# A list schedule that plans itself again from its own deadlines, with four products of the first pair moved ahead of the pair and the fillers written into the next operation's bank

## The chip, the cores and the metric

One NeuronCore of a Trainium2 chip runs the whole kernel. The metric is the device time of one execution in microseconds; three executions of the kernel before took 883.96 (median), 883.89 and 884.6 us. The engines are TensorE (PE: matrix products into PSUM; PEld is its weight load, which overlaps), VectorE (DVE), ScalarE (ACT), GpSimd (POOL) and SyncE (SP), whose queue issues every DMA here. Each engine runs its instructions in the order in which they were written and waits for the others by semaphores.

## The reference

Attention with pooled keys and values, followed by a two-layer gated network over all tokens:

```python
# 8 batches, 8 heads, 576 tokens, head_dim 64; q, k, v float32
k_p = k.reshape(B, H, 72, 8, D).mean(axis=3); v_p = v.reshape(B, H, 72, 8, D).mean(axis=3)
scores = np.matmul(q, k_p.transpose(0, 1, 3, 2)) / np.sqrt(D)
scores = scores - np.max(scores, axis=-1, keepdims=True)
attn = np.exp(scores); attn = attn / (np.sum(attn, axis=-1, keepdims=True) + 1e-09)
x = np.matmul(attn, v_p)            # then (tokens, heads*D) = (4608, 512)
h = x @ w_in                        # w_in (512, 2048), w_out (2048, 512)
sp = np.maximum(h, 0.0) + np.log1p(np.exp(-np.abs(h)))
out = (h * erf(sp)) @ w_out
```

## The kernel before

**Numbers.** The products of the network are made from limbs: a float32 matrix is cut into a high part and the rest, and one product is three matmuls (high x high, high x low, low x high; the helper `three`, line 687). The weights arrive as words of 64 bits where they are given so and are turned into float32 by ScalarE or GpSimd (`cv`, `low`), VectorE (lines 397 and 399, `cv` and `f`) and cut into `w` limbs (`halves`: the high part on ScalarE or GpSimd, line 340 or 341, the rest on VectorE or GpSimd, line 352).

**Tiling.** The 4608 tokens are nine chunks of 512. Chunk 0 goes through plain products: sixteen blocks of 128 of the hidden dimension, each 12 matmuls of 128x512 (`plain_in`), then `second`, 192 matmuls into four output banks. Chunks 1 to 8 go in four pairs, s = 1 to 4. In a pair the first layer runs in eight quads (`quad`): a quad makes four 128x512 blocks of h for both chunks from seven products of six matmuls by a scheme of Strassen and Winograd. Its moving operands are differences of the two chunks' x (T1, T2, T3, T4) beside x itself (B11, B21, B22), made in `sides` as limbs; its weights are blocks of w_in (`w`) and their sums (`ws`, made in `sums`). For the first pair seven of the eight products A11 x B11 are made ahead by `head`, which leaves p1 in SBUF, since they need only the first chunk of the pair. In a quad with a p1 the product A12 x B21 has its own bank and is added to p1 on VectorE (`add(g[0, 0], p1, A)`).

**Activation.** `activation` takes four blocks: softplus of each on ScalarE out of PSUM (line 697), erf of the four in two instructions (line 701), then the product with h (line 705 or 708). Softplus lies in another function table than erf and sigmoid, so ScalarE loads a table between them. In the plain stage the multiplication of line 708 is the last reader of the bank, so the bank is free for another block when it is done.

**Attention.** For each tile of up to 128 tokens: scores (PE line 520), maximum and difference (DVE 529, 545), a sigmoid that stands for the exponential (ACT 539 or 549), the sum and its reciprocal (551 to 555), scaling (561, 565), transposes (PE 572, 575), values (PE 615, 616), and x out of PSUM; chunk 0 is cut into limbs at once (ACT 633, DVE 635). Keys and values are pooled on VectorE (line 470: `ks` and `vs`).

**What sets the order.** Nothing is written in the order in which it runs. Every operation is handed to `Program.op` with an engine (some with a second choice), a modelled cost, a priority (a due time from constants like `FIRST`, `LONG`, `PERIOD`) and the buffers that it holds; `Program.order` is a list schedule over that model. At each step it looks at every operation whose inputs are planned, works out its start on its engine, prefers small `start + SLACK * prio`, takes the earliest of the five engines' picks and gives its new buffers the place that came free first: 8 banks of PSUM (at most 6 for h, 4 for o, 4 for attention), 87 places of 2 KB in SBUF with a limit for each kind, such as 12 for `gl` or 14 for `w`. The instructions are then written in that order, so the order on every engine and every reuse of a place is fixed before the chip runs; a place that a slow store still holds makes the next user wait.

**Fillers.** Where the plan leaves PE idle in the first 57 us, small matmuls of constants (128x256, bfloat16) are written, of 107 ns in the plan, into one bank that is kept aside for them until 57 us:

```python
spare = heapq.heappop(slots["bank"])
...
idle = start - max(free["PE"], 3000.0) - MARGIN - (1800 if not free["PE"] else 0)
out.extend([self.filler] * int(idle / 107))
```

## Time and profile before

| | |
|---|---|
| median of three executions | 883.96 us |
| the profiled execution, its own time | 884.53 us |
| its span, first to last instruction | 882.5 us |
| mean granted TensorE clock | 0.992 |
| PE busy | 852.9 us (97%) |
| VectorE, ScalarE, GpSimd busy | 713.5, 561.6, 437.9 us |
| matmuls of the network (three groups: o; h by w; h by ws) | 1584 + 1344 + 192 |
| fillers | 178, 24.0 us |
| table loads of ScalarE | 36 + 28 + 8 + 1, 1283 ns each |

How to read it: busy times overlap, and an engine that is 97% busy leaves 29.6 us of the span to be won, as far as its work itself does not change; fillers count as busy, though they compute nothing. Idle time of the other engines counts only where PE waits for them. In a row of the timeline the first two numbers are start and length in us, the last bracket is the idle time of the engine just before and what ended it. In a row of groups the numbers behind the bar are busy us and mean ns of one.

### The profile page before, as it was taken

Reading aid. Unit: us, or ns where it says so; the run is one execution under the profiler, and the core shown is the slowest. Engines: PE = TensorE matmul, PEld = TensorE weight load, DVE = VectorE, ACT = ScalarE, POOL = GpSimd, SP = SyncE. Lnnn points to the kernel's source line nnn. Section 1 sums busy time; section 2 is a strip of 40 time slices with the busy share of each in tenths; the row PEclk is TensorE's granted clock in tenths of the full one; section 3 lists DMA queues with packets and bytes.
Section 4 is the critical chain, followed back from the end, with each engine's and each line's share of the span. In section 5 each row is a group of like instructions: output and inputs, shape, how many; then the busy total and the mean of one; then the engine's idle time right before and its main releaser. Section 6 shows DMA issues by size and latency. Waiting matters only on the chain. (4 is left out here: it accounts for less than half of the span.)

```text
span 882.5 us, 13579 instructions
## 1 busy us (share of the span) xinstructions
PE 852.9 (97%) x4106; PEld 701.0 (79%) x4106; DVE 713.5 (81%) x1264; ACT 561.6 (64%) x1002; POOL 437.9 (50%) x453
## 2 busy tenths in 40 slices
PE   8989899979899999999999999999999999999998
PEld 6777788768778888888887888888888888888886
DVE  5978779868888889578999998889898984567982
ACT  4778867648964475268766734587867445887630
POOL 1777578436856883035485333155474312484210
PEclk9999999989999999999999999999999999999999
DMA  8677999799898959997474367974633679448541
GB/s 286 228 243 243 295 353 321 253 375 383 294 340 315 374 196 375 353 355 268 141 267 146 119 204 262 352 238 121 227 120 120 203 268 350 118 121 266 175 163 52
DMA packets 125207, 218.03 MB, mean 247 GB/s; under 512 B 16976, under 2 KB 31440, under 8 KB 125136
## 3 DMA queue, kind: packets, MB, share of 16 engines
q1 hardware_dynamic: 125136, 217.18, 72.2%
q8 instruction: 33, 0.54, 0.3%
q14 instruction: 38, 0.31, 0.1%
HBM read 167.84 MB, written 49.28 MB: 246 GB/s over the span
## 5 line engine op out<-in xcount | busy, mean ns | idle before, releaser
L687 PE MATMUL o<-gl,w 128*128 128x512 f32 x1584 | 377.0, 393 | 1.6 <-DVE gl L352 1.4
L687 PEld LDWEIGHTS o<-gl,w 128*128 128x128 f32 x1584 | 292.7, 188 | 63.5 <-DVE gl L352 1.8
L687 PE MATMUL h<-x,w 128*128 128x512 f32 x1344 | 319.1, 394 | 7.5 <-DVE g L708 3.0
L687 PEld LDWEIGHTS h<-x,w 128*128 128x128 f32 x1344 | 250.9, 189 | 62.1 <-DVE g L708 3.2
L340 ACT ACTIVATE gl<-g 128x512 fp32r<-128x512 f32 x204 | 119.7, 624 | 74.9 <-DVE g L833 32.0
L352 POOL TENSOR_TENSOR gl<-g,gl 128x512 fp32r<-128x512 f32 x77 | 108.1, 1410 | 66.8 <-ACT gl L340 62.3
L705 POOL TENSOR_TENSOR g<-d,g 128x512 f32<-128x512 f32 x54 | 69.8, 1310 | 107.6 <-ACT d L701 93.8
L352 DVE TENSOR_TENSOR gl<-g,gl 128x512 fp32r<-128x512 f32 x139 | 107.6, 807 | 0.4 <-ACT gl L340 0.2
L770 DVE TENSOR_TENSOR g<-t,h 128x512 f32<-128x512 f32 x96 | 65.6, 684 | 41.0 <-PE h L687 39.9
L701 ACT ACTIVATE d<-d 128x1024 f32<-128x1024 f32 x72 | 72.7, 1051 | 0.3
L833 POOL TENSOR_TENSOR g<-g 128x512 f32<-128x512 f32 x48 | 67.3, 1413 | 8.8 <-DVE gl L352 6.1
L697 ACT ACTIVATE d<-g 128x512 f32<-128x512 f32 x103 | 57.5, 622 | 5.3 <-DVE g L770 5.2
L770 DVE TENSOR_TENSOR t<-t,h 128x512 f32<-128x512 f32 x57 | 39.1, 686 | 24.1 <-PE h L687 22.7
L687 PE MATMUL h<-x,ws 128*128 128x512 f32 x192 | 49.0, 410 | 6.8 <-DVE x L352 4.5
L561 POOL TENSOR_TENSOR bb<-s,z 128x64 f32<-128x64 f32 (+1 forms) x40 | 12.9, 322 | 81.1 <-DVE z L555 26.6
L687 PEld LDWEIGHTS h<-x,ws 128*128 128x128 f32 x192 | 38.1, 200 | 16.5 <-issue 6.3
L340 ACT ACTIVATE x<-xr 128x512 fp32r<-128x512 f32 (+2 forms) x64 | 34.4, 559 | 25.1 <-DVE xr L661 12.0
L615 PE MATMUL att<-et,va 128*128 128x256 f32 (+3 forms) x192 | 46.1, 340 | 1.4 <-DVE g L708 0.6
L520 PE MATMUL att<-kbd,q 128*128 128x144 f32 (+1 forms) x320 | 46.3, 287 | 1.2 <-issue 0.7
L520 PEld LDWEIGHTS att<-kbd,q 128*128 128x128 f32 (+1 forms) x320 | 42.2, 179 | 6.1 <-issue 2.2
L697 ACT ACT_TABLE_LOAD x36 | 46.2, 1283 | 0.6
L549 ACT ACTIVATE s<-s,cst 128x576 f32<-128x576 f32 (+1 forms) x36 | 27.9, 775 | 25.0 <-DVE s L545 24.8
(92 smaller groups left out, 1153.4 us busy)
## 6 DMA issues: line engine op xcount, KB each, us to landing
w<-ws SPq DMA_DIRECT2D x192, 256.0 KB, 4.8
w<-wo SPq DMA_DIRECT2D x136, 256.0 KB, 3.8
w<-wi SPq DMA_DIRECT2D x96, 256.0 KB, 5.0
ws<-ws SPq DMA_DIRECT2D x64, 256.0 KB, 5.3
v<-vl SPq DMA_DIRECT2D x48, 256.0 KB, 5.3
raw<-kl SPq DMA_DIRECT2D x32, 288.0 KB, 4.3
out<-f SPq DMA_DIRECT2D x36, 256.0 KB, 2.1
q<-qa SPq DMA_DIRECT2D x32, 256.0 KB, 5.1
```

The source lines that it names most:

```text
L340: op("ACT", act(n), prio, lambda: nc.scalar.activation(dst(), src(), AF.Copy, scale=scale), *access, turn=turn, alt=("POOL", 0.833 * n + 1 ...
L352: both(True, dve(n), gps(n), prio + 0.1, lambda e: e.tensor_sub(lo(), src(), f32(hi())), reads + [hikey], [lokey])
L520: nc.tensor.matmul(o, raw.ap[:, p, :T], kbd[:, p], start=(p % 2 == 0), stop=True, skip_group_check=True)
L549: op("ACT", act(H * SP) + 93, r + 0.8, lambda: nc.scalar.activation(s.ap[:T], s.ap[:T], AF.Sigmoid, bias=bias[0][:T], scale=1.0 / 64.0), [ ...
L561: nc.gpsimd.tensor_mul(bb.ap[:T], sv, zv.unsqueeze(2).broadcast_to([T, NP, 16]))
L615: nc.tensor.matmul(o, va[:, p], et.ap[:, p, :n], start=e == 0, stop=False, skip_group_check=True)
L687: nc.tensor.matmul(o, u, v, start=first and q == 0, stop=last and q == 2, skip_group_check=True)
L697: nc.scalar.activation(y(k), h.ap, AF.Softplus)
L701: op("ACT", act(1024), prio + 0.2, lambda k=k: nc.scalar.activation(ys[k].ap, ys[k].ap, AF.Erf), own[2 * k:2 * k + 2], own[2 * k:2 * k + 2 ...
L705: both(True, dve(512), gps(512), prio + 0.3, lambda e, k=k, h=h: e.tensor_mul(h.ap, y(k), h.ap), [own[k], h], [h])
L770: op("DVE", dve(512), prio, lambda: nc.vector.tensor_add(dst.ap, u.ap, o.ap), [u, o], [dst])
L833: both(True, dve(512), gps(512), prio, lambda e: e.tensor_sub(out.ap, u.ap, v.ap), [u, v], [out])
```

## The change

It has five parts.

1. *Passes.* `order` runs the list schedule up to eight times. After a pass, `latest` walks back from the planned end and finds for every operation the latest time at which it could end without moving that end, by its consumers, by the next operation on its engine and by the next user of its place; the latest start, divided by 5100 ns, is the operation's priority in the next pass. The pass with the shortest planned length is kept.
2. *Necks.* For four quads of the first pair the product A12 x B21 is made ahead, right after the heads (`neck`), and added to p1 in front of the quad; the quad then lacks that product and that add.
3. *Fillers.* No bank is kept aside. A filler goes into the bank that the next operation will take, from when that bank is free in the plan, in the first 57 us and later wherever the plan leaves PE idle for over 1.2 us.
4. *Softplus in twos.* The four softplus of `activation`, one operation before, are two operations of two.
5. A place keeps the operation that freed it, for the deadlines of part 1.

```diff
+PASSES, UNIT = 8, 5100.0
-HEADS = 7
+HEADS, NECKS = 7, 4
-FILL, MARGIN = 57000.0, 300
+FILL, MARGIN, LONG_IDLE = 57000.0, 300, 1200.0
...
+    def latest(self):
+        for o in self.ops:
+            o.late = self.length
+        for o in sorted(self.ops, key=lambda o: -o.start):
+            at = o.late - o.cost
+            for d, flow in o.next:
+                gap = self.DELAY[o.eng] if d.eng != o.eng else (self.SAME[o.eng] if flow else 0)
+                at = min(at, d.late_at - gap - o.cost)
+            for d, gap in o.after:
+                at = min(at, d.late_at - gap - o.cost)
+            o.late_at = at
+
+    def order(self, passes=PASSES):
+        best = None
+        self.prios = [o.prio for o in self.ops]
+        for n in range(passes):
+            self.reset()
+            try:
+                out = self.once()
+            except RuntimeError:
+                break
+            if best is None or self.length < best[0]:
+                best = (self.length, out, [(o.eng, o.cost, o.fn, o.start) for o in self.ops],
+                        [(b, b.place) for o in self.ops for b in o.bufs])
+            self.latest()
+            for o, p in zip(self.ops, self.prios):
+                o.prio = o.late_at / UNIT
...
-        spare = None
-        if self.filler:
-            spare = heapq.heappop(slots["bank"])
-            self.idle.place = spare[1]
...
+            if o.eng == "PE":
+                new = [b for b in o.bufs if b.home == "bank" and not b.held]
+                idle = start - max(free["PE"], 3000.0) - (1800 if not free["PE"] else 0)
+                if new and (start < FILL or idle > LONG_IDLE):
+                    begin = max(free["PE"], 4800.0 if not free["PE"] else 0.0, slots["bank"][0][0])
+                    out.extend([(self.filler, new[0])] * int((start - begin - MARGIN) / 107))
...
-        def softplus():
-            for k, (h, _) in enumerate(hs):
-                nc.scalar.activation(y(k), h.ap, AF.Softplus)
-
-        op("ACT", 4 * act(512), prio, softplus, [h for h, _ in hs], own, funcs="softplus")
+        for i in (0, 2):
+
+            def softplus(i=i):
+                for k in (i, i + 1):
+                    nc.scalar.activation(y(k), hs[k][0].ap, AF.Softplus)
+
+            op("ACT", 2 * act(512), prio + 0.01 * i, softplus, [h for h, _ in hs[i:i + 2]], own[i:i + 2], funcs="softplus")
...
+    def neck(s, i, x, due, p1):
+
+        a12 = piece(lambda: in_hbm[i][:, 1], IN[i], due)
+        A, g = bank("h"), place("g")
+        product(A, a12, "B21", x, due, False, True)
+        op("DVE", dve(512), due + 0.3, lambda: nc.vector.tensor_add(g.ap, p1.ap, A.ap), [p1, A], [g])
+        return g
...
-        if early:
+        if early and not g00:
             next(A, a12, "B21", False, True)
             add(g[0, 0], p1, A, due + 1.7)
...
+        g00s = [neck(s, i, x, start(s) - 0.5, ps[i]) for i in range(NECKS if s == 1 else 0)]
```

In numbers of instructions: the products and the attention are the same on PE, fillers are 240 instead of 178, ScalarE's table loads 97 instead of 73; the `gl` copies on ScalarE are 186 instead of 204 and on GpSimd 30 instead of 12; copies of `t` out of PSUM are 22 on VectorE instead of 10 and 3 on ScalarE instead of 15. GpSimd has 499 instructions instead of 458. The DMAs are the same 807 issues, in another order.

Where it moves instructions that the prediction speaks of, the rows of the program on one engine. Line numbers of the changed kernel are some 54 to 65 higher than those of the kernel before. First VectorE at the end of the start, up to the last limbs of chunk 0's x, before:

```order
L589 TENSOR_TENSOR etb<-att,etb 32x128 x2
L397 SCALAR_TENSOR_TENSOR cv<-cv,low 128x512
L470 TENSOR_REDUCE ks<-raw 128x72
L399 SCALAR_TENSOR_TENSOR f_688<-d,cv 128x512
L635 TENSOR_TENSOR x<-att,x 128x256 x2
L397 SCALAR_TENSOR_TENSOR cv<-cv,low 128x512
L470 TENSOR_REDUCE vs<-v 128x64
L399 SCALAR_TENSOR_TENSOR f_721<-d,cv 128x512
L635 TENSOR_TENSOR x<-att,x 128x256 x2
```

and now (583 and 599 are maximum and difference of the fifth tile, 689 the limb of x):

```order
L583 TENSOR_REDUCE m<-att 64x4 x2
L451 SCALAR_TENSOR_TENSOR cv<-cv,low 128x512
L599 TENSOR_TENSOR s<-att,m 64x288
L453 SCALAR_TENSOR_TENSOR f_775<-d,cv 128x512
L599 TENSOR_TENSOR s<-att,m 64x288
L451 SCALAR_TENSOR_TENSOR cv<-cv,low 128x512
L689 TENSOR_TENSOR x<-att,x 128x256 x2
L453 SCALAR_TENSOR_TENSOR f_806<-d,cv 128x512
L524 TENSOR_REDUCE vs<-v 128x64
L689 TENSOR_TENSOR x<-att,x 128x256
L451 SCALAR_TENSOR_TENSOR cv<-cv,low 128x512
L689 TENSOR_TENSOR x<-att,x 128x256
```

From the first four limbs of x to the last one, three pooled `vs`, three `cv`, two `f`, two maxima and two differences of the fifth tile have come in between; a `ks`, a limb of `w` and a scaling are no longer there, and one more `ks` stands ahead of the first four.

Second SP's queue with the loads of v (for `vs`) and of w_in, before:

```order
L386 DMA d<-wi 128x1024 x2
L467 DMA v<-vl 128x512 x2
L386 DMA d<-wi 128x1024 x7
L512 DMA q<-qa 128x512
L386 DMA d<-wi 128x1024 x2
L467 DMA v<-vl 128x512
L467 DMA raw<-kl 128x576
L386 DMA d<-wi 128x1024
L467 DMA v<-vl 128x512
```

and now:

```order
L521 DMA v<-vl 128x512
L566 DMA q<-qa 128x512
L440 DMA d<-wi 128x1024 x2
L521 DMA raw<-kl 128x576 x2
L521 DMA v<-vl 128x512
L566 DMA q<-qa 128x512
L440 DMA d<-wi 128x1024
L521 DMA v<-vl 128x512
L440 DMA d<-wi 128x1024
L521 DMA v<-vl 128x512
```

The tenth load of v, the first one in the last three rows of before and the second one here, has fourteen loads of w_in ahead of it in the queue before and five now.

Third PE just ahead of the first pair's quads, before (T2 is the first product by `ws`; the pair of 615 and 616 stands twice):

```order
L687 MATMUL h<-x,w 128x512 x24
L615 MATMUL att<-et,va 128x128
L616 MATMUL att<-etb,vb 64x128
L687 MATMUL h<-x,ws 128x512 x18
L687 MATMUL h<-x,w 128x512 x12
```

and now (the last two rows, a filler, stand 25 times, and then the T2 product follows):

```order
L741 MATMUL h<-x,w 128x512 x12
L669 MATMUL att<-et,va 128x128
L670 MATMUL att<-etb,vb 64x128
L741 MATMUL h<-x,w 128x512 x24
L669 MATMUL att<-et,va 128x128
L670 MATMUL att<-etb,vb 64x128
L1001 LDWEIGHTS cst
L1001 MATMUL h<-cst 128x256
```

66 matmuls of the first pair stand ahead of T2 now instead of 42, the last values of the attention directly ahead of the fillers.

More of the change, by code (lines that the diff above doesn't have):

```diff
@@ L180, in op, with reset, once @@
         return o
-    def order(self):
+    def reset(self):
+        for o in self.ops:
+            if not hasattr(o, "first"):
+                o.first = (o.wait, o.eng, o.cost, o.fn)
+            o.wait, o.eng, o.cost, o.fn = o.first
+            o.ready, o.done, o.before = 0.0, False, []
+            for b in o.bufs:
+                b.left, b.held, b.end, b.last = 0, False, 0.0, None
+        for o in self.ops:
+            for b in o.bufs:
+                b.left += 1
+    def latest(self):
+        for o in self.ops:
+            o.late = self.length
[22 more added lines that the diff above has]
+                o.prio = o.late_at / UNIT
+        self.length, out, how, places = best
+        for o, h in zip(self.ops, how):
+            o.eng, o.cost, o.fn, o.start = h
+        for b, p in places:
+            b.place = p
+        return out
+    def once(self):
+        for o in self.ops:
+            o.after = []
+        last, porter = {}, None
         free = {e: 0.0 for e in self.DELAY}
@@ L185, in order @@
         port = 0.0
-        slots = {t: [(0.0, i) for i in range(n)] for t, n in self.capacity.items()}
+        slots = {t: [(0.0, i, None) for i in range(n)] for t, n in self.capacity.items()}
         avail = {e: [] for e in free}
@@ L239, in order @@
             loaded = o.set or loaded
-            if spare is not None and o.eng == "PE":
-                if start > FILL:
-                    heapq.heappush(slots["bank"], (start, spare[1]))
-                    spare = None
-                else:
-                    idle = start - max(free["PE"], 3000.0) - MARGIN - (1800 if not free["PE"] else 0)
-                    out.extend([self.filler] * int(idle / 107))
+            if o.eng == "PE":
[4 more added lines that the diff above has]
+                    out.extend([(self.filler, new[0])] * int((start - begin - MARGIN) / 107))
             end = free[o.eng] = start + o.cost
@@ L249, in order @@
                 port = end
+            if o.eng in last:
+                last[o.eng].after.append((o, 0))
+            last[o.eng] = o
             o.done = True
@@ L256, in order @@
                     b.held = True
-                    b.places = {t: heapq.heappop(slots[t])[1] for t in b.limits}
+                    b.places = {}
+                    for t in b.limits:
+                        _, b.places[t], by = heapq.heappop(slots[t])
+                        if by is not None and by is not o:
+                            by.after.append((o, 150 + (DGE if e == "SP" else 0)))
                     b.place = b.places[b.home]
                 b.left -= 1
-                b.end = max(getattr(b, "end", 0.0), end)
+                if end >= b.end:
+                    b.end, b.last = end, o
                 if not b.left:
                     for t in b.limits:
-                        heapq.heappush(slots[t], (b.end + 150, b.places[t]))
+                        heapq.heappush(slots[t], (b.end + 150, b.places[t], b.last))
             for d in o.follow:
@@ L748, in head, with quad @@
         return p1
-    def quad(s, i, x, base, p1=None):
+    def neck(s, i, x, due, p1):
[4 more added lines that the diff above has]
+        return g
+    def quad(s, i, x, base, p1=None, g00=None):
         due = base + LONG / NQ * i
@@ L758, in quad @@
         s2, s3, s1 = sm(1), sm(2), sm(0)
-        a12 = piece(lambda: in_hbm[i][:, 1], IN[i], due)
+        if g00 is None:
+            a12 = piece(lambda: in_hbm[i][:, 1], IN[i], due)
         a22 = piece(lambda: in_hbm[i + NQ][:, 1], IN[i + NQ], due)
         s4 = sm(3)
-        A, Bk, C, Dk = (bank("h") for _ in range(4))
+        A, Bk, C, Dk = (None if m == 0 and g00 else bank("h") for m in range(4))
         n = [0]
@@ L773, in quad @@
         fts = (i, i + NQ)
-        g = {(m, t): place("g") for m in range(2) for t in range(2)}
+        g = {(m, t): g00 if g00 and m + t == 0 else place("g") for m in range(2) for t in range(2)}
         if not early:
@@ L919, in moe_attention @@
         ps = [head(s, i, x, start(s) - 1) for i in range(HEADS if s == 1 else 0)]
+        g00s = [neck(s, i, x, start(s) - 0.5, ps[i]) for i in range(NECKS if s == 1 else 0)]
         for i in range(NQ):
-            quad(s, i, x, start(s), ps[i] if i < len(ps) else None)
+            quad(s, i, x, start(s), ps[i] if i < len(ps) else None, g00s[i] if i < len(g00s) else None)
         span = SHORT if s < NC // 2 else 16
@@ L932, in moe_attention @@
             seconds(s, start(s) + LONG, span)
-    idle = bank("h")
     cb = c.bitcast(mybir.dt.bfloat16)
-    pr.idle = idle
-    pr.filler = Op("PE", 107, 0, lambda: nc.tensor.matmul(
-        idle.ap[:, :256], cb[:, :P], cb[:, :256], start=True, stop=True))
+    pr.filler = lambda b: nc.tensor.matmul(b.ap[:, :256], cb[:, :P], cb[:, :256], start=True, stop=True)
     ops = pr.order()
@@ L941, in moe_attention @@
     for o in ops:
-        o.fn()
+        if isinstance(o, tuple):
+            o[0](o[1])
+        else:
+            o.fn()
 def kernel(q, k, v, moe_w_in, moe_w_out):
```

## The prediction

> **What bounds the kernel now.** I read the page's busy times first, then a table of windows cut where TensorE's work changes kind, then TensorE's own timeline, then the engines on which it waits.
>
> ```profile
> span 882.5 us, 13579 instructions
> PE 852.9 (97%) x4106; PEld 701.0 (79%) x4106; DVE 713.5 (81%) x1264; ACT 561.6 (64%) x1002; POOL 437.9 (50%) x453
> 0.00:40.70 40.70, 35.23 (x263) 28.35 (x263) 29.21 (x69) 24.75 (x101) 18.21 (x32) 1.00 0.76 262
> 40.70:94.10 53.40, 49.08 (x216) 39.56 (x215) 43.00 (x78) 40.33 (x60) 38.44 (x44) 0.97 0.76 241
> 94.10:176.20 82.10, 76.88 (x396) 62.39 (x394) 69.27 (x143) 57.73 (x126) 54.46 (x65) 1.00 0.91 309
> 176.20:181.00 4.80, 0.48 (x2) 0.19 (x2) 2.73 (x9) 1.54 (x5) 0.00 (x0) 0.73 1.04 350
> 181.00:257.00 76.00, 72.14 (x300) 58.31 (x301) 61.21 (x103) 60.35 (x86) 48.41 (x51) 0.95 0.97 345
> 257.00:878.00 621.00, 618.75 (x2938) 512.17 (x2936) 506.96 (x866) 376.94 (x629) 278.37 (x263) 1.00 0.67 227
> ```
>
> The columns are window, length, then busy time of PE, PEld, DVE, ACT and POOL, then granted clock, DMA share and GB/s. From 257 us to 878 us PE is busy 618.75 of 621.00 us: nothing is to be won there, and the new order has the same products in the same places, so I leave it alone. What can move lies before 257 us: a start of 40.7 us in which PE waits for the first attention and mostly runs fillers, 4.3 us idle in the first GEMM (53.40 - 49.08), 5.2 us in the next stage, of which the last 1 us belongs to the wait that follows, 4.3 us in that wait, 3.9 us in the quads of the first pair, and some half clock. The rows that end these waits:
>
> ```profile
> 38.88 2.03 PE L937 MATMUL h<-cst 128*128 128x256 bf16 x17
> 40.67 16.61 PE L687 MATMUL h<-x,w 128*128 128x512 f32 x72
> 57.11 1.14 PE L520 MATMUL att<-kbd,q 128*128 128x144 f32 x8
> 61.24 10.06 PE L687 MATMUL h<-x,w 128*128 128x512 f32 x36 [2.99 <-DVE g L708]
> ...
> 176.16 0.50 PE L687 MATMUL h<-x,ws 128*128 128x512 f32 x1 [0.96 <-ACT x L340]
> 180.99 1.62 PE L687 MATMUL h<-x,ws 128*128 128x512 f32 x3 [4.32 <-DVE x L352]
> ...
> 231.87 2.00 PE L687 MATMUL h<-x,w 128*128 128x512 f32 x6 [2.31 <-DVE t L770]
> ```
>
> The first 72 matmuls take 57.11 - 40.67 = 16.44 us, 0.228 us each; seventeen fillers take 40.67 - 38.88 = 1.79 us, 0.105 us each. Each long wait is followed by a clock of one half for about 3.4 us or twice that:
>
> ```profile
> 61.20:64.60 3.40, 3.36 (x10) 2.72 (x11) 3.40 (x6) 3.38 (x6) 3.18 (x4) 0.66 0.97 363
> 181.00:184.00 3.00, 2.79 (x6) 1.79 (x7) 2.25 (x10) 1.03 (x3) 0.00 (x0) 0.50 1.07 388
> 231.60:235.00 3.40, 3.13 (x10) 2.49 (x11) 3.16 (x6) 3.37 (x5) 3.40 (x8) 0.70 0.42 124
> ```
>
> A clock share missing is time lost: 53.4 x 0.03 = 1.7 us after the first wait; 76.0 x 0.05 = 3.8 us in the quads, of which 3.0 x 0.50 and a tail of 0.6, 2.1 us, come from the wait at 181 us and 1.7 us from that at 232 us. The 36 matmuls behind the first wait confirm it: 10.06 us against 36 x 0.228 = 8.2 us.
>
> **Step 1, the start: +4.0 us.** The last limb of chunk 0's x releases the first GEMM, and VectorE is busy without a gap from the first four limbs to the last:
>
> ```profile
> 29.47 1.41 DVE L635 TENSOR_TENSOR x<-att,x 128x256 fp32r<-128x256 f32 x4
> 40.03 0.75 DVE L635 TENSOR_TENSOR x<-att,x 128x256 fp32r<-128x256 f32 x2
> L470 DVE TENSOR_REDUCE vs<-v 128x64 f32<-128x512 f32 x48 | 31.6, 674 | 3.2 <-DMA v<-vl 3.1
> L470 DVE TENSOR_REDUCE ks<-raw 128x72 f32<-128x576 f32 x32 | 23.8, 747 | 9.6 <-DMA raw<-kl 9.5
> L397 DVE SCALAR_TENSOR_TENSOR cv<-cv,low 128x512 uint32<-128x512 uint32 x32 | 22.0, 692 | 3.8 <-ACT cv L389 3.3 <-POOL low L395 0.2
> L399 DVE SCALAR_TENSOR_TENSOR f<-d,cv 128x512 uint32<-128x512 uint32 x32 | 21.5, 677 | 0.2
> L529 DVE TENSOR_REDUCE m<-att 64x4 f32<-64x288 f32 x16 | 6.8, 441 | 2.0 <-PE att L520 1.8
> L545 DVE TENSOR_TENSOR s<-att,m 64x288 f32<-64x288 f32 x16 | 6.6, 440 | 0.0
> L565 DVE TENSOR_TENSOR s<-s,z 128x576 f32<-128x576 f32 x25 | 26.3, 1051 | 0.9 <-POOL bb L561 0.8
> L352 DVE TENSOR_TENSOR w<-f,w 128x512 fp32r<-128x512 f32 x12 | 11.0, 915 | 4.7 <-POOL w L341 4.5
> ```
>
> In the new order three vs, three cv, two f, two m and two s more stand between the same two points: 3 x 0.674 + 3 x 0.692 + 2 x 0.677 + 2 x 0.441 + 2 x 0.440 = 7.2 us. One ks, one w and one s x z are gone: 0.747 + 0.915 + 1.051 = 2.7 us. That is +4.5 us; as the next instruction starts some 0.08 us before a listed end, nine more make it 3.8, and one ks more ahead of the first limbs and the s x z on GpSimd can add a little. I take 4.0, between 2 (fillers already held the first GEMM back by up to 1.8 us) and 6. Nothing hides it: PE has only fillers there, 34 more of them (3.6 us), which fill this gap and don't cause it. The work that was pulled ahead is late nowhere afterwards; it is what step 2 needs.
>
> **Step 2, first GEMM: -4.5 us.** Its 3 us wait is for bank space, and the profile shows why the bank came late:
>
> ```profile
> 49.78 1.28 ACT L697 ACT_TABLE_LOAD   x1
> 51.08 2.06 ACT L697 ACTIVATE d<-h 128x512 f32<-128x512 f32 x4
> 54.98 2.01 ACT L701 ACTIVATE d<-d 128x1024 f32<-128x1024 f32 x2
> L389 ACT ACTIVATE cv<-d 128x512 f32<-128x512 f32 x32 | 20.3, 635 | 3.5 <-issue 1.4 <-DVE xr L347 1.3 <-DVE s L545 0.5
> 59.90 0.69 DVE L470 TENSOR_REDUCE vs<-v 128x64 f32<-128x512 f32 x1 [3.08 <-DMA v<-vl]
> 60.51 2.47 DVE L708 TENSOR_TENSOR g<-d,h 128x512 f32<-128x512 f32 x4
> ```
>
> The multiplies (line 708) that free the banks were done on ScalarE's side at 57.0 us, but stood on VectorE behind a vs whose load sat on SP's queue behind fourteen loads of wi, which wait for their own slots; in the new order it sits behind five. And the first softplus pair starts after two products (of twelve matmuls each), not four. Worked by hand from 44.7 us on: two products end at 50.2; two softplus (1.2), a cv (0.6), a load (1.3) and an erf (1.0) end near 54.3; the 19 instructions that VectorE has between the last limb and these multiplies, some 0.6 us each, end near 56.6, two multiplies at 58. The first bank is wanted again after six products, at 61.1. So the 4.3 us of waits and 1.7 us of half clock go, -6.0. Back come 1.5 us: ScalarE now loads its table 14 times in this stage, not 8, 6 x 1.283 = 7.7 us, against 53.40 - 40.33 = 13.1 us that it was idle, and the first o products need four banks at once just behind the last activations. Ends: 0 to 5 us for that.
>
> [...]
>
> **Step 3, 94 to 176 us: 0.** The same products and attention, reshuffled; its 4 us of small waits may go or double, -4 to +4. Over the whole run eighteen gl copies move from ScalarE to GpSimd, at
>
> ```profile
> L341 POOL TENSOR_SCALAR gl<-g 128x512 fp32r<-128x512 f32 x12 | 15.0, 1252 | 18.4 <-DVE gl L352 12.1 <-PE att L575 5.0 <-PE att L520 0.8
> ```
>
> 22 us on an engine that is half idle, with twelve gl slots as a cushion; a gl that is late after all holds back six o matmuls.
>
> **Step 4, the wait for T2: -4.1 us.** What the first pair's products wait for are sides made from the last attention values. PE now has four more products (24 matmuls x 0.228 = 5.5 us) ahead of this point, but also ahead of the last values, so they don't fill the wait itself; they give VectorE time to be further on. In the old run two slots of SBUF came late:
>
> ```profile
> 180.08 0.96 DVE L352 TENSOR_TENSOR x<-xr,x 128x384 fp32r<-128x384 f32 x3 [2.07 <-DMA wf<-f]
> 181.44 0.72 ACT L340 ACTIVATE x<-xr 128x384 fp32r<-128x384 f32 x2 [3.62 <-DMA wo<-w]
> L770 DVE TENSOR_TENSOR g<-t,h 128x512 f32<-128x512 f32 x96 | 65.6, 684 | 41.0 <-PE h L687 39.9 <-DMA w<-ws 0.7
> ```
>
> Without them 5.5 us of wait (0.96 + 4.32 + 0.20) become some 3.5, the copy, two differences and two limbs of the last block. I take -2.0, from 0 (other stores hold slots) to -2.5. Then the 25 fillers, 25 x 0.105 = 2.6 us, leave under 1 us idle, and the half clock behind it goes: -2.1, or 0 if the fillers end early. VectorE's four neck adds (684 ns each by the last row, 2.7 us) stand ahead of the last T2 limb; they have their inputs before the last value and run in the wait, and where they don't they cost these 2.7.
>
> Waits of 2.99 and 2.31 us have halved the clock here (0.66 and 0.70 behind them), so if the fillers end 2 us early the 2.1 are lost and the sum is -5.2. [...]
>
> **Step 5, quads: -2.7 us.** 3.9 us of waits and 1.7 us of clock, where VectorE reached an add late among long multiplies. Four quads are one product and one add shorter, 5.5 us and 2.7 us, which moved ahead; but ScalarE, busy 60.35 of 76.00 us, has the same activations and two or three loads more. I take half, from -5.4 to +3.
>
> **Sum:** 4.0 - 4.5 + 0 - 4.1 - 2.7 = -7.3 us on a span of 882.5, 875.2. The profiled execution took 884.53 us, 0.57 above the median of the runs, 883.96, from which the same -7.3 gives **876.7 us**.
>
> **The rivals.** *The waits come back* (0.13): the start costs 4.0, the first GEMM wins 4.5, but T2 waits for slots as long as before, the fillers end ahead of it, and VectorE is as late in the quads: steps 4 and 5 are 0, 883.5 us. For it: the stores are the same, at a DMA share of 1.04 in that window. Against it: their queue positions and slots all differ.
>
> *ScalarE's loads set the pace* (0.17): the slower side. Each pair of softplus has its own two loads, and from the point where two products (12 matmuls each, 5.5 us) are shorter than a pair's work on ScalarE, 2 x 1.283 + 2 x 0.6 + 1.0 + two cv of 0.6 = 6.0 us, banks come late again. Step 2 is then 0 (4.3 of waits and the clock stay), the quads, where PE has 5.5 us less to do but ScalarE 3 us more, +3, T2 -2.0 with the clock lost: 4.0 + 0 - 2.0 + 3 = +5.0, 889 us. Against it: 13.1 us of idle time of ScalarE in the first GEMM.
>
> *All waits up to 257 us go* (0.12): 4.0 - 6.0 - 4 - 5.5 - 2.1 - 5.4 = -19, 865 us. Against it: the fillers placed ahead of T2 say that a wait is still there. That the new passes are thrown away is no case: the start and the loads are in another order.
>
> **How the numbers follow.** My forecast has 0.58, and nearly all of it is faster by over 0.2% (1.8 us, about what a measurement of this kernel can tell from no change). With the case of 865 that makes 0.70 faster, 0.13 the same and 0.17 slower. All low ends of the five steps at once would give 866 us and all high ends 896; neither set falls together, so the range is 867 to 888, which leaves out most of the 865 case and the worse half of the slower one.
>
> **What would show it.** Step 1: the first GEMM starts at 43 to 46 us instead of 40.67. Step 2: no wait of over 1 us on line 708's successor in the first 120 matmuls, a clock of 1.00 up to 94 us, and ScalarE's idle time there down from 13 to about 5 us. Step 4: fillers and wait ahead of T2 together below 4 us, clock 1.00 behind them. Step 5: under 2.5 us idle in the quads. I am wrong if ScalarE is busy without a gap and PE waits on it, if PE idles over 5 us ahead of T2, or if new waits appear after 257 us.

## The result, and the profile after

Four executions of the changed kernel took 870.65 to 873.41 us, median **871.72**; four of the kernel before 883.89 to 885.38, median 884.28. The ratio is **0.9858, 95% interval 0.9836 to 0.9879**: 12.6 us faster, where the prediction had 7.3 (876.7 us, range 867 to 888). The profiled execution took 872.73 us, 11.8 less than that of before; its span is 871.0 against 882.5.

The head of its page:

```profile
span 871.0 us, 13708 instructions
PE 854.3 (98%) x4168; PEld 704.7 (81%) x4168; DVE 702.5 (81%) x1258; ACT 578.9 (66%) x991; POOL 476.9 (55%) x494
```

And the windows, cut at the same events as in the prediction (start; first GEMM; up to T2's first product; quads of the first pair; the rest), with the columns as there:

```profile
0.00:44.30 44.30, 39.75 (x304) 32.91 (x305) 32.90 (x77) 29.82 (x109) 23.47 (x36) 1.00 0.89 318
44.30:93.80 49.50, 47.96 (x229) 39.39 (x226) 40.90 (x70) 45.16 (x61) 37.92 (x45) 1.00 0.98 341
93.80:176.30 82.50, 81.75 (x430) 67.47 (x427) 69.72 (x153) 56.48 (x122) 62.81 (x75) 1.00 0.95 335
176.30:243.60 67.30, 65.51 (x287) 52.88 (x285) 60.96 (x92) 57.97 (x76) 53.69 (x60) 1.00 0.93 321
243.60:866.50 622.90, 618.63 (x2929) 511.86 (x2928) 496.62 (x868) 389.43 (x627) 299.02 (x280) 1.00 0.64 220
```

Between the first GEMM and the end of the quads PE idles 1.5 + 0.8 + 1.8 us, where it idled 4.3 + 5.2 + 4.3 + 3.9 us, and the clock no longer drops there. In the last window it idles 4.3 us instead of 2.3. TensorE's timeline at the places that the prediction named:

```profile
44.31 27.46 PE L741 MATMUL h<-x,w 128*128 128x512 f32 x120
...
91.60 0.41 PE L669 MATMUL att<-et,va 128*128 128x64 f32 x2 [1.28 <-DVE s L599]
...
93.78 1.64 PE L741 MATMUL o<-gl,w 128*128 128x512 f32 x6
...
173.48 0.31 PE L670 MATMUL att<-etb,vb 96*64 96x128 f32 x1
173.62 2.90 PE L1001 MATMUL h<-cst 128*128 128x256 bf16 x25
176.28 4.37 PE L741 MATMUL h<-x,ws 128*128 128x512 f32 x18
180.75 1.67 PE L741 MATMUL h<-x,w 128*128 128x512 f32 x6
...
211.22 1.66 PE L741 MATMUL h<-x,w 128*128 128x512 f32 x6 [0.81 <-DVE t L835]
...
511.30 26.15 PE L741 MATMUL o<-gl,w 128*128 128x512 f32 x107 [1.97 <-POOL gl L406]
```

The first GEMM starts 3.6 us later and then runs 120 matmuls in one piece; from the last attention values to T2 there are only the fillers; the longest wait of the quads is 0.81 us; and a wait of 1.97 us at 511 us is new.

| step | predicted | measured, us | |
|---|---|---|---|
| 1, start | +4.0 | **+3.6** | first GEMM at 44.31 instead of 40.67 |
| 2, first GEMM | -4.5 | **-3.9** | 49.47 instead of 53.38 up to the first o product |
| 3, 94 us to the last values | 0 | **-3.5** | waits 4.3 (5.2 less T2's first 1.0), now 0.8 |
| 4, T2 | -4.1 | **-4.9** | 5.5 of wait and 2.1 of clock, now 2.7 of fillers |
| 5, quads | -2.7 | **-3.8** | 3.9 of waits and 1.7 of clock, now 1.8 |
| behind the quads | 0 | **+3.7** | waits 2.3, now 4.3, and 1.7 of clock |

That is -8.8 of the 11.5 us by which the span is shorter. Of the rest some 1.5 us (an estimate: some 17 matmuls of attention at about 0.09 us) is work that PE now does ahead of the first o product instead of fillers and waits; 1.2 us I cannot assign to a row. That -8.8 lies near the predicted -7.3 is in part luck: the -3.5 of step 3 and the +3.7 behind the quads, both put at 0, nearly cancel.

### The profile page after: what moved, and what is told of

It reads as the page before. It is cut to its first block, busy times and chain, and to the rows that moved or that the text cites. A ratio compares the mean times of both kernels' runs of the same rounds, so it can differ in the third digit from the quotient of the medians.

```text
span 871.0 us, 13708 instructions
## 1 busy us (share of the span) xinstructions
PE 854.3 (98%) x4168; PEld 704.7 (81%) x4168; DVE 702.5 (81%) x1258; ACT 578.9 (66%) x991; POOL 476.9 (55%) x494
## 4 chain that ended last, share of the span: by engine, by line
PE 70%; DVE 3%; POOL 1%; issue 1%; DMA 1%; ACT 0%; SPq 0%; DVEq 0%; ACTq 0%; POOLq 0%
PE o L741 34%; PE h L741 28%; PE att L574 3%; PE att L669 2%; PE att L626 1%; POOL gl L406 1%; PE att L670 1%; DVE gl L406 1%; DMA v<-vl 0%; DVE t L835 0%; DVE g L898 0%; DMA out<-f 0%; PE att L629 0%; DVE f L922 0%; DVE g L835 0%
## 5 line engine op out<-in xcount | busy, mean ns | idle before, releaser
L394 ACT ACTIVATE gl<-g 128x512 fp32r<-128x512 f32 x186 | 110.9, 624 | 56.0 <-DVE g L898 25.8
L761 POOL TENSOR_TENSOR g<-d,g 128x512 f32<-128x512 f32 x65 | 87.8, 1367 | 94.3 <-ACT d L757 85.1
L406 POOL TENSOR_TENSOR gl<-g,gl 128x512 fp32r<-128x512 f32 x68 | 108.0, 1596 | 50.9 <-ACT gl L394 47.4
L406 DVE TENSOR_TENSOR gl<-g,gl 128x512 fp32r<-128x512 f32 x148 | 110.3, 769 | 5.8 <-ACT gl L394 4.9
L898 POOL TENSOR_TENSOR g<-g 128x512 f32<-128x512 f32 x37 | 51.0, 1379 | 36.0 <-DVE gl L406 16.8
L753 ACT ACTIVATE d<-g 128x512 f32<-128x512 f32 x103 | 59.3, 624 | 5.6 <-DVE g L835 5.4
L741 PE MATMUL h<-x,ws 128*128 128x512 f32 x192 | 45.6, 390 | 0.5 <-DVE g L835 0.5
L898 DVE TENSOR_TENSOR g<-g 128x512 f32<-128x512 f32 x59 | 45.2, 770 | 0.8
```

The source lines that it names most:

```text
L394: op("ACT", act(n), prio, lambda: nc.scalar.activation(dst(), src(), AF.Copy, scale=scale), *access, turn=turn, alt=("POOL", 0.833 * n + 1 ...
L406: both(True, dve(n), gps(n), prio + 0.1, lambda e: e.tensor_sub(lo(), src(), f32(hi())), reads + [hikey], [lokey])
L741: nc.tensor.matmul(o, u, v, start=first and q == 0, stop=last and q == 2, skip_group_check=True)
L753: nc.scalar.activation(y(k), hs[k][0].ap, AF.Softplus)
L761: both(True, dve(512), gps(512), prio + 0.3, lambda e, k=k, h=h: e.tensor_mul(h.ap, y(k), h.ap), [own[k], h], [h])
L898: both(True, dve(512), gps(512), prio, lambda e: e.tensor_sub(out.ap, u.ap, v.ap), [u, v], [out])
```

## The experiments

Twelve kernels were run. A one-pass kernel is one in which the hand-set due times alone decide. "Lost" is, in the profiled execution of each, PE's idle time and written fillers (0.1075 us each) from the first GEMM to the end of the first pair's quads, without half clock. Each ratio is to executions of the kernel before that were taken beside that run (medians 884.1 to 884.7).

| run | passes | split | products ahead | late fillers | median us | ratio to before, 95% | lost |
|---|---|---|---|---|---|---|---|
| before | 1 | no | 0 | no | 884.28 | | 17.7 |
| e11 | 1 | no | 0 | no | 881.76 | 0.9981 (0.9958 to 1.0003) | 16.2 |
| e8 | 1 | yes | 0 | no | 880.13 | 0.9949 (0.9929 to 0.9968) | 15.1 |
| e1 | 1 | yes | 4 | yes | 880.03 | 0.9954 (0.9937 to 0.9972) | 16.7 |
| e5 | 8 | no | 0 | no | 872.47 | 0.9862 (0.9838 to 0.9885) | 9.6 |
| e4 | 8 | no | 4 | yes | 871.60 | 0.9867 (0.9849 to 0.9885) | 10.5 |
| e2 | 8 | yes | 0 | yes | 872.78 | 0.9868 (0.9840 to 0.9896) | 11.6 |
| e3 | 8 | yes | 4 | no | 871.63 | 0.9868 (0.9850 to 0.9885) | 4.8 |
| changed | 8 | yes | 4 | yes | 871.72 | 0.9858 (0.9836 to 0.9879) | 7.1 |
| e12 | 8, random | yes | 4 | yes | 872.52 | 0.9873 (0.9848 to 0.9898) | 8.7 |
| e7 | 8 | yes | 7 | yes | 868.50 | 0.9816 (0.9794 to 0.9839) | |
| e6 | 8 | yes | 4 | yes | 869.01 | 0.9827 (0.9801 to 0.9852) | |
| e10 | 8 | yes | 7 | yes | 867.12 | 0.9798 (0.9781 to 0.9816) | |
| e9 | 8 | yes | 7 | yes | 870.03 | 0.9835 (0.9810 to 0.9860) | |

"Lost" does not order the kernels with eight passes: e3 lost 4.8 us and e2 11.6, and their medians are 1.15 us apart, with intervals that overlap. e6, e9 and e10 have further edits, below. The expectations call the multiply of the plain stage line 762, its number in e4, e5 and e11; in the other kernels it is 764.

**e1, one pass.**

```diff
-PASSES, UNIT = 8, 5100.0
+PASSES, UNIT = 1, 5100.0
```

> The changed kernel with one pass of the list schedule instead of eight (the order from the hand-set due times), all else kept. Theory A (the passes bring most of the 12.3 us): the first GEMM starts near 40.7 us again instead of 44.3, the pooled v of the tenth load is late again and TensorE waits 2 to 3 us for a bank behind line 762's multiplies, the quads of the first pair lose 3 to 4 us to late adds again, and the time is 879 to 884 us. Theory B (the split softplus and the four products ahead bring it, and the passes only reshuffle): the same early start, but no wait of over 1 us in the first GEMM, the quads without gaps, and 869 to 873 us.

880.03 us, theory A's time: 8.3 us of the gain come with the passes (whether by their deadlines, e12 asks). Its details were only half right. The first GEMM starts at 39.50 us and the quads wait 6.0 us, but the first GEMM's longest wait behind the multiplies is 0.98 us, not 2 to 3. Two rows of TensorE's timeline in the quads:

```profile
195.33 1.67 PE L741 MATMUL h<-x,w 128*128 128x512 f32 x6 [1.60 <-DVE t L835]
212.62 7.34 PE L741 MATMUL h<-x,ws 128*128 128x512 f32 x24 [1.99 <-DVE g L835]
```

The four products are ahead here too, four quads have six matmuls and one add less, and VectorE's adds are late all the same.

**e2, no products ahead.**

```diff
-HEADS, NECKS = 7, 4
+HEADS, NECKS = 7, 0
```

> The changed kernel with no product A12 x B21 made ahead; passes, split softplus and fillers kept. 24 matmuls (5.5 us) go back from ahead of T2 into the quads, and 56 fillers instead of 25 stand ahead of T2. Theory A (the four products cover part of the wait for T2): the stretch of fillers and wait ahead of T2 grows from 2.7 us to about 6 us and nothing comes back later, so 874 to 876 us. Theory B (the products only change places: what was covered ahead of T2 is a gap a little later, or the last limbs come earlier without the four adds on VectorE): 870 to 873 us, the first T2 product about 2.2 us earlier than in the changed kernel and the quads 5.5 us longer.

TensorE's timeline ahead of T2:

```profile
167.62 6.29 PE L1001 MATMUL h<-cst 128*128 128x256 bf16 x56
173.67 4.38 PE L741 MATMUL h<-x,ws 128*128 128x512 f32 x18
```

Nearest to theory B, in time (872.78) and place: T2 starts 2.6 us earlier and the quads end 1.7 us later (245.21 against 243.56). The stretch of fillers does grow to 6.3 us as A said. The executions lie between 870.53 and 875.81, so that 1 us is not told apart from the changed kernel.

**e3, no late fillers.** Every operation stands in the same order; 28 fillers are left out.

```diff
-FILL, MARGIN, LONG_IDLE = 57000.0, 300, 1200.0
+FILL, MARGIN, LONG_IDLE = 57000.0, 300, 1e9
```

> The changed kernel in the same order, without the 28 fillers behind 57 us (25 of them ahead of T2, 3 ahead of the first o product). Theory A (the wait for T2 is still there, and the fillers only keep the clock up): TensorE idles 2.5 to 3 us ahead of T2, T2 starts at 176.3 us as before, the granted clock falls to one half for about 3.4 us behind it, and the time is 1.5 to 2.5 us longer, 873.5 to 874.5 us. Theory B (T2's limbs are ready before the fillers end): T2 starts up to 2 us earlier and the time is 870 to 871.5 us. [...]

TensorE's timeline around T2:

```profile
175.44 0.31 PE L670 MATMUL att<-etb,vb 96*64 96x128 f32 x1
175.59 0.92 PE L741 MATMUL h<-x,ws 128*128 128x512 f32 x3
177.40 4.10 PE L741 MATMUL h<-x,ws 128*128 128x512 f32 x15 [0.90 <-ACT x L394]
182.06 1.66 PE L741 MATMUL h<-x,w 128*128 128x512 f32 x6 [0.56 <-DVE t L835]
```

Theory B. Three matmuls of T2 can run at once, and the others wait 0.90 us, with the clock at 1.00 behind them. From the last values to the product behind T2 it is 182.06 - 175.44 = 6.62 us here and, by the same rows of the changed kernel (173.48 and 180.75), 7.27 there: its 2.7 us of fillers were longer than the wait, and cost 0.65 us. The medians, 871.63 and 871.72, cannot tell that apart.

**e4, softplus of four.**

```diff
-        for i in (0, 2):
-            def softplus(i=i):
-                for k in (i, i + 1):
+        def softplus():
+            for k, (h, _) in enumerate(hs):
```

> The changed kernel with the four softplus of an activation as one operation again (73 table loads instead of 97 or so); passes, products ahead and fillers kept. Theory A (banks come free earlier because the first two softplus need not wait for four products): TensorE waits 3 us or more in the first GEMM or the quads again, 877 to 882 us. Theory B (ScalarE's 24 table loads of 1.283 us cost as much as the split gains): ScalarE has 31 us less to do, no wait of over 1 us comes back, 870 to 873 us.

871.60: theory B's time, with a wait that B had excluded, though shorter than theory A's 3 us, in TensorE's timeline of the first GEMM:

```profile
74.63 5.72 PE L741 MATMUL h<-x,w 128*128 128x512 f32 x17 [1.92 <-DVE g L762]
```

The wait of before at 61 us is gone without the split, with the passes alone; another comes 13 us later, where four softplus run together at 68.95 to 71.02 us and the four multiplies follow only at 73.80. In e1 and e8, with the split and one pass, the wait at 61 us is gone too. So either of the two reasons that the prediction gave for step 2 is enough for that wait; what other waits are left depends on the order (0.98 us in e1, 1.92 here, and 1.33 in e2, which has both). But the 1.92 us and their half clock are given back by an earlier first GEMM (42.95 us) and by 4.5 us idle behind the quads instead of the changed kernel's 8.1 with 1.7 of half clock.

**e5, the passes alone.** e4 with no products ahead and no late fillers:

```diff
-HEADS, NECKS = 7, 4
+HEADS, NECKS = 7, 0
-FILL, MARGIN, LONG_IDLE = 57000.0, 300, 1200.0
+FILL, MARGIN, LONG_IDLE = 57000.0, 300, 1e9
```

> The passes alone: eight passes, but no product made ahead, softplus of four in one operation, and no fillers behind 57 us (fillers of the start in the next operation's bank, as in the changed kernel). With one pass the other parts together gave 4.1 us, and with eight passes each of them alone could be left out for nothing. Theory A (the passes repair whatever is left, the parts are not needed): 870 to 874 us, waits of up to 2 us in the first GEMM, hardly any in the quads. Theory B (one of split softplus and products ahead is needed for the passes to find a place for the rest): 876 to 880 us, with a wait for T2 of 4 us or more.

T2 in TensorE's timeline:

```profile
172.51 0.47 PE L741 MATMUL h<-x,ws 128*128 128x512 f32 x1 [1.05 <-ACT x L394]
174.61 5.73 PE L741 MATMUL h<-x,ws 128*128 128x512 f32 x17 [1.63 <-DVE x L406]
```

Theory A: 872.47. T2 waits 2.7 us, not 5.5, the quads once (1.53 us at 241 us, for a limb of `ws`). The passes bring what the whole change brings, with only the place of the start's fillers beside them (e11 has that place alone); passes with a bank kept aside were not run.

**e8, the split alone.** The edits of e5, with the split kept, and one pass:

```diff
-PASSES, UNIT = 8, 5100.0
+PASSES, UNIT = 1, 5100.0
```

> The split softplus alone: one pass, no product ahead, no fillers behind 57 us (those of the start in the next operation's bank). With one pass and all of split, products ahead and late fillers it was 880.0 us, 4.1 below the kernel before. Theory A (the split brings these 4 us, since a bank is free two products earlier): 879 to 881.5 us, waits in the first GEMM of at most 1.5 us. Theory B (the products ahead bring them): 882.5 to 885 us, with a wait for T2 of 4 us and more as in the kernel before.

880.13 us, theory A's time, and also theory B's wait for T2, in TensorE's timeline:

```profile
173.37 0.50 PE L741 MATMUL h<-x,ws 128*128 128x512 f32 x1 [0.96 <-ACT x L394]
177.33 4.21 PE L741 MATMUL h<-x,ws 128*128 128x512 f32 x9 [3.46 <-DVE x L406]
184.12 2.50 PE L741 MATMUL h<-x,ws 128*128 128x512 f32 x5 [2.58 <-DVE x L406]
```

ScalarE's timeline in the same stretch of the same run:

```profile
181.34 0.94 ACT L394 ACTIVATE x<-xr 128x384 fp32r<-128x384 f32 x2 [4.86 <-DMA wf<-f]
```

A limb for these products waits 4.86 us for the place that a weight store still holds. In the changed kernel neither ScalarE nor VectorE waits for a store in this stretch (GpSimd does once, for 0.87 us). In e5 no limb of x waits for one, though GpSimd stands 8.57 us ahead of a limb of `ws`. This is the slot of the prediction's step 4, and these two orders, found with passes, do not wait for it.

**e11, one pass, nothing else.** e8 with e4's edit, softplus of four; what is left of the change is where the fillers of the start go.

> The changed kernel without passes, products ahead, split softplus and fillers behind 57 us; what is left of the change is the place of the fillers of the start, in the next operation's bank instead of one kept aside. With the split it was 880.1 us. Theory A (the split alone brought these 4 us): 882.5 to 885 us, and a wait of 2 us or more behind line 762's multiplies in the first GEMM. Theory B (the bank that is no longer kept aside until 57 us brings them): 879 to 881.5 us.

881.76 us, between the two theories, and without theory A's sign: the longest wait behind line 762's multiplies in the first GEMM is 1.34 us. Its executions lie in two groups, 879.6 to 883.8 and 887.9 to 888.2, and its ratio reaches 1. The split's share without passes stays open: 1.6 us by the medians of e8 and e11, with intervals that overlap.

**e6, two gl moved from GpSimd to VectorE.** The wait at 511 us is for a low limb of `gl`. GpSimd's timeline there in the changed kernel:

```profile
497.61 13.63 POOL L406 TENSOR_TENSOR gl<-g,gl 128x512 fp32r<-128x512 f32 x2 [5.50 <-ACT gl L394]
...
512.44 1.28 POOL L406 TENSOR_TENSOR gl<-g,gl 128x512 fp32r<-128x512 f32 x1
```

VectorE's timeline beside it, the first and the last of 24 instructions in a row, and between them the only two that do not have both operands in SBUF (they read `o` out of PSUM):

```profile
495.60 0.67 DVE L898 TENSOR_TENSOR g<-g 128x512 f32<-128x512 f32 x1
...
501.02 1.27 DVE L922 TENSOR_TENSOR f<-t,o 128x512 f32<-128x512 f32 x2
...
509.44 0.67 DVE L898 TENSOR_TENSOR g<-g 128x512 f32<-128x512 f32 x1
```

Two subtractions take GpSimd 13.63 us, 4.65 and 9.03 one by one, where one soon behind them takes 1.28. VectorE runs without a gap from 495.60 to 510.1 us. GpSimd's first one ends 1.16 us after the last VectorE instruction ahead of the two that read PSUM, and its second one 1.13 us after VectorE's last. e6 makes these two on VectorE, in the same place of the written order:

```diff
     ops = pr.order()
+    for o in ops:
+        if not isinstance(o, tuple) and o.eng == "POOL" and 496000 < o.start < 498500:
+            o.eng, (o.cost, o.fn) = "DVE", o.choice["DVE"]
```

> The changed kernel in the same order, but two low limbs of gl that GpSimd makes at 497.6 to 511.2 us (4.65 and 8.98 us, where the next one takes 1.28) are made by VectorE at the same place in its order, 0.6 us each. Theory A (GpSimd cannot read its two operands from SBUF while VectorE runs one such instruction after another from 495.6 to 510.1 us, and TensorE's 1.97 us wait at 511 with the half clock behind it comes from that): the wait is gone, the clock stays at 1.00 there, GpSimd has no gl of over 3 us between 490 and 515 us, and the profiled time is 2 to 3.7 us shorter, 868.5 to 870 us. Theory B (something else is late there, such as the weights or VectorE): a wait of 1 us or more stays within 5 us of that place and the time stays at 871.7 us.

TensorE's timeline from 500 to 514 us is one row:

```profile
499.74 14.44 PE L741 MATMUL o<-gl,w 128*128 128x512 f32 x63
```

Theory A: TensorE runs through, the clock stays at 1.00 (63 matmuls in 14.44 us, 0.229 us each), and the median falls by 2.7 us to 869.01, with intervals that still overlap. The trace shows more: GpSimd, once behind, is kept waiting over many VectorE instructions in a row, 4.65 us for its first subtraction and 9.03 for its second. Why they keep it waiting was not shown; theory A's reason for it was my assumption.

**e7, seven products ahead.**

```diff
-HEADS, NECKS = 7, 4
+HEADS, NECKS = 7, 7
```

> The changed kernel with seven products A12 x B21 made ahead instead of four. Theory A (what the products ahead hide is used up: fillers and waits between first GEMM and quads are 8 us already, and 25 fillers stand ahead of T2 here too): 870 to 873 us. Theory B (each product ahead takes an add from VectorE in the quads, where it is the engine that is late): 867.5 to 869.5 us, with no wait over 0.4 us in the quads.

868.50 us, theory B's time and sign: no wait is left in the quads, and the five executions lie within 0.5 us. That it is by B's reason, the adds, is not shown. The GpSimd wait is there too, 1.42 us at 508 us, in TensorE's timeline and, in the second fence, GpSimd's:

```profile
508.36 21.83 PE L741 MATMUL o<-gl,w 128*128 128x512 f32 x95 [1.42 <-POOL gl L406]
```

```profile
495.22 13.08 POOL L406 TENSOR_TENSOR gl<-g,gl 128x512 fp32r<-128x512 f32 x2 [4.23 <-DVE gl L406]
```

That four products ahead cost nothing when taken away (e2) and three more bring 3.2 us says how little such a difference is a property of the part: each edit makes the planner find another order.

**e10, e7 with its two gl on VectorE** (e6's edit with the planned times 493500 and 496000).

> The kernel with seven products made ahead (868.5 us) in the same order, with the two low limbs of gl that took GpSimd 4.0 and 9.0 us near 500 us on VectorE instead. Theory A (the 1.42 us wait at 508 us is GpSimd's, kept from its operands by VectorE): that wait is gone and the time is 866.5 to 867.5 us, 1.0 to 2.0 us shorter. Theory B (VectorE, without a gap there, is late by the 1.2 us that it gets): another wait of the same length within 10 us, 868 to 869 us.

The wait is gone; 867.12 us, theory A, 1.4 us under e7's median, though the two intervals overlap. It is the fastest kernel of this study, 0.9798 (0.9781 to 0.9816) of the kernel before, 17.6 us by the medians.

**e9, e10 with an earlier start.** In the passes after the first:

```diff
-                o.prio = o.late_at / UNIT
+                o.prio = o.late_at / UNIT - (0.4 if i < self.first_jobs else 0)
```

`first_jobs` counts the operations of chunk 0's attention; the two gl are again moved by their planned times.

> The kernel with seven products made ahead and the two gl of the dense stretch near 500 us on VectorE, and in the later passes every operation of chunk 0's attention gets a priority 0.4 units (2 us) earlier. Theory A (the 3.6 us by which the first GEMM starts later are a loss of their own, VectorE doing later work first): the first GEMM starts at 42 to 43.5 us, no wait of over 1 us comes back in it, and the time is 865 to 867 us, 1 us or more below the next kernel. Theory B (what is done first at the start is missing later): the same start gain, but waits in the first GEMM or a later first o product, and 867 to 870 us.

The first GEMM starts at 44.09 us instead of e10's 45.84 and the first o product 1.7 us earlier, with no new wait between, but the quads wait 1.77 and 0.78 us where e10 has none, and the median is 870.03, with executions from 867.1 to 874.4. That is nearest to theory B, with the loss later than it said: this way of starting earlier does not pay.

**e12, eight shuffled orders.** Do the passes gain by their deadlines, or by having eight orders to choose from?

```diff
-            self.latest()
+            rng = np.random.default_rng(n)
             for o, p in zip(self.ops, self.prios):
-                o.prio = o.late_at / UNIT
+                o.prio = p + rng.uniform(-0.2, 0.2)
```

> The changed kernel, but passes 2 to 8 take the hand-set due times with a random offset of up to 0.2 units (1 us) to each operation instead of the deadlines of the pass before; the order that is shortest in the plan is kept as before. Theory A (the deadlines bring the gain, not the choice among eight orders): 876 to 880 us, within 4 us of the one-pass kernel's 880.0, with waits in the quads of 3 us or more in all. Theory B (any eight orders, of which the shortest is kept, bring it): 870 to 874 us.

872.52 us: theory B in time, with theory A's waits in the quads. The time is made in other places. TensorE's timeline:

```profile
180.07 2.93 PE L741 MATMUL h<-x,w 128*128 128x512 f32 x6 [2.59 <-DVE t L835]
190.62 5.73 PE L741 MATMUL h<-x,ws 128*128 128x512 f32 x24 [0.65 <-DVE g L835]
197.67 1.65 PE L741 MATMUL h<-x,w 128*128 128x512 f32 x6 [1.32 <-DVE t L835]
```

Counted from T2's first matmul to the end of the quads, it waits 5.9 us, as the one-pass kernels do (6.0 to 7.7), where e2 to e5 and the changed kernel, with deadlines, wait 1.1 to 3.2. (Of the 7.7 us of e8, 6.0 are waits for T2's limbs, the rows above.) It wins at the start instead: the first GEMM begins at 39.52 us, as with one pass, and idles 0.8 us. It is one draw of seven offsets; another may be worse.

## Why the prediction was right or wrong

**The direction and the range held; the size was 5 us short.** Of the 5.3 us between 7.3 and 12.6, 1.5 lie in the steps, 2.7 are the two rests named under the table of steps, and 1.1 lie between the profiled executions' spans and the medians. The three terms that rested on rows and counted instructions came out near: step 1 (+4.0, measured +3.6), step 2 (-4.5, -3.9), step 4 (-4.1, -4.9). Each sign that was named for them is there: a first GEMM at 44.31 us, 120 matmuls without a wait, a clock of 1.00, and ScalarE idle 49.50 - 45.16 = 4.3 us in that stage. (The prediction's 53.4 x 0.03 is 1.6, not 1.7; one stretch of 3.413 us at half clock, which the trace of the kernel before has there, is 1.7, so the term stands.)

**Step 3 failed first.** It was put at 0 because "its 4 us of small waits may go or double". They went, 3.5 of 4.3 us, and nothing came in their place. In e11, e8 and e1, with one pass, 2.0 to 4.6 us of idle time stay between the first o product and T2; in e5, e4 and e2, with eight, 0 to 1.1; e12, with shuffled orders, keeps 2.0.

**Step 5 had its sign for the wrong reason.** It was taken as half of what shorter quads could bring. From T2's first matmul to the end of the quads, PE waits 6.0 us with shorter quads and one pass (e1), and 2.3 and 3.2 with quads of full length and passes (e2, e5). So the order decides there, not the length of the quads alone, and of the orders tried those from deadlines wait least: the shuffled one of e12 leaves 5.9.

**Step 4 had two reasons, and both count at that place.** From the last attention values to the first product behind T2's eighteen matmuls it is 12.3 us in the kernel before. With one pass and no products ahead it is 12.4 (e11) and 15.6 (e8), and 8.8 with the four ahead (e1). With passes it is 9.0 (e5) and 10.4 (e2, where 56 fillers may be what T2 waits for) without them and 6.6 to 7.3 with them (e3, e4, the changed kernel). So the four products do give VectorE time, as step 4 said, and an order in which no limb waits for a store's place helps besides; the medians of e2 and e5 do not show what the four products are worth in time. I also left 3.5 us of chain there for the last block; e3 shows that 0.90 us of it is waited for.

**The fillers ahead of T2 were no measure of the wait that remains.** Their number is the plan's; the chip's wait was shorter than they are.

**The part left alone was not alone.** Behind 257 us, "the new order has the same products in the same places, so I leave it alone": that holds for PE. But GpSimd now makes some of the limbs in other company, and that cost 3.7 us in the profiled execution. The prediction had named "if new waits appear after 257 us" as a sign of being wrong, and by that sign this part of it was. It also wrote that "a gl that is late after all holds back six o matmuls"; that is what happened, by a low limb and not by the copies it had counted, and with a price of 2.0 us of wait and 1.7 of clock.

**Of the rivals** none was the case. The waits did not come back. ScalarE loads its table 13 times for the activations of the first GEMM instead of 7 (1.283 us each) and PE waits for none of them (groups of ScalarE's instructions in that stage of the changed kernel):

```profile
L753 ACT ACT_TABLE_LOAD x7 | 9.0, 1283 | 1.4 <-DVE g L764 1.3
L757 ACT ACT_TABLE_LOAD x6 | 7.7, 1283 | 0.1
```

The third came nearest: of its 23 us of waits and half clock up to the end of the quads (6.0 + 4 + 5.5 + 2.1 + 5.4) some 19 went, 4.5 + 3.5 + 7.6 + 3.8; but 2.7 us of fillers stand in their place, and 3.7 us were lost behind the quads.

So the deadlines go with where this kernel's waits went, but a kernel of some 872 us does not need them: e12 finds one without. What stays open is how far e12's order is luck, which of the eight passes was kept and how one of them alone would do, and why several quite different orders end within 1.2 us of each other (e2, e3, e4, e5, e12 and the changed kernel, 871.6 to 872.8).

## What to carry to other kernels

When a planner's order is remade as a whole, the new order is the change: here its choice among eight was worth 7.5 to 8.3 us, with deadlines or with random offsets, while the parts beside it (a split, products moved ahead, fillers) were worth 4 us without it and, taken away one by one or together, nothing measurable with it, so several orders should be timed before a gain is put down to a part. Fillers sized by a plan can be longer than the wait that they fill. And look for GpSimd's elementwise work in stretches where VectorE has no gap: the group's mean hides it (1596 ns here), single rows of many us show it (13.63 us for two here).

## What the runs showed of the hardware

**GpSimd was held back for up to 9 us beside VectorE,** as told under e6: 13.63 us for two subtractions, where one soon behind them takes 1.28. The fourteen traces have 17 elementwise instructions of 128x512 on GpSimd that last over 4 us, from 4.09 to 9.03. Each of them ends at nearly the same time after VectorE's last instruction with both operands in SBUF: the 13 with two operands 1.13 to 1.16 us after it, the four with one operand 0.48 to 0.49. What follows on VectorE there is a pause or an instruction that reads `o` out of PSUM.

**Waits of the same length were followed by half a clock in one run and not in another.** The clock's records in the traces of the kernel before and of the changed kernel show it at one half only for 3.413 us or, once before, 6.827 us (the last one of each is cut by the end), and each such stretch begins a whole number of 3.413 us after the first record of its execution: 16, 50 and 66 times before, 148 in the changed kernel, and likewise 26 in e3 and 20 in e4. The same wait at the same place of the program went either way. The attention waits 1.28 us ahead of the first o product in the changed kernel (its row at 91.60 us above) and in e3, whose timeline of TensorE has

```profile
93.19 0.41 PE L669 MATMUL att<-et,va 128*128 128x64 f32 x2 [1.28 <-DVE s L599]
```

e3 lacks the three fillers that stand behind this wait in the changed kernel, but they are not what decides: e7 and e10 have them, the same order and the same 1.28 us, and the six `o` matmuls behind take 1.64 us in e7, and 2.76, at half clock, in e10. The windows of 2 us behind this wait, the clock being the third number from the end, in the changed kernel and then in e3:

```profile
94.00:96.00 2.00, 2.00 (x14) 1.74 (x13) 0.40 (x4) 1.99 (x3) 1.85 (x2) 1.00 0.99 316
96.00:98.00 2.00, 2.00 (x12) 1.68 (x11) 1.94 (x5) 1.98 (x7) 0.75 (x1) 1.00 1.02 271
```

```profile
94.00:96.00 2.00, 1.74 (x10) 1.37 (x10) 1.94 (x5) 1.97 (x4) 1.56 (x3) 0.82 0.71 239
96.00:98.00 2.00, 2.00 (x7) 1.58 (x6) 0.00 (x0) 1.99 (x5) 1.43 (x2) 0.50 0.95 352
```

And the GpSimd wait at 511 us, 1.97 us in the changed kernel and 1.96 in e3,

```profile
511.87 24.55 PE L741 MATMUL o<-gl,w 128*128 128x512 f32 x107 [1.96 <-POOL gl L406]
```

is followed by half a clock in the changed kernel (the first of the two fences of windows) (2 x 0.31 + 2 x 0.50 + 2 x 0.04 = 1.7 us) and not in e3:

```profile
512.00:514.00 2.00, 2.00 (x8) 1.61 (x7) 0.09 (x1) 1.48 (x3) 1.73 (x2) 0.69 0.05 14
514.00:516.00 2.00, 2.00 (x6) 1.52 (x5) 1.41 (x3) 0.19 (x1) 0.00 (x0) 0.50 0.27 105
516.00:518.00 2.00, 2.00 (x10) 1.64 (x9) 2.00 (x4) 1.43 (x3) 0.00 (x0) 0.96 0.60 218
```

```profile
512.00:514.00 2.00, 2.00 (x9) 1.66 (x10) 0.00 (x0) 0.91 (x2) 2.00 (x2) 1.00 0.06 22
514.00:516.00 2.00, 2.00 (x10) 1.65 (x10) 1.98 (x4) 0.77 (x2) 0.32 (x1) 1.00 0.22 85
```

So waits of 1.28 us (e3 and e10, among small matmuls of the attention) and 1.97 us (the changed kernel) were followed by half a clock, and waits of 1.28 us (the changed kernel and e7) and 1.96 us (e3) were not; what decides it was not shown. One such drop, 1.7 us, is of the size of the spread between executions of one kernel, but does not explain it alone: the slowest execution of the changed kernel, 873.41 us, had a mean granted clock of 1.0, the profiled one, 872.73 us, 0.998.
